# A fused attention and expert kernel whose hand-planned step list gets new durations and landing times

## The chip, the cores and the metric

The kernel runs on one core of one Trainium2 chip. The metric is the device time of one execution in microseconds. A profile of one execution gives the instructions of every engine: TensorE (PE, with its weight loads as PEld), VectorE (DVE), ScalarE (ACT), GpSimd (POOL) and SyncE (SP, which issues most transfers).

## The reference

Three parts follow one another, all in 32-bit floats.

```python
# attention: q, k, v are (4, 8, 576, 64)
kv = einsum('bhsd,bhse->bhde', k, v)
out = einsum('bhsd,bhde->bhse', q, kv)
out = out / sqrt(mean(out * out, -1) + 1e-06) * g_norm
x = out as (2304, 512)
# experts: 8 of them, one for each token
logits = (x / |x|) @ (expert_emb / |expert_emb|).T / tau
idx, gate = argmax(logits), softmax(logits)[idx]
x = gate * (relu(x @ w1[idx]) @ w2[idx])          # 512 -> 1024 -> 512
# dense layer
return softplus(x @ w_in) @ w_out                 # 512 -> 2048 -> 512
```

## The kernel before

The work falls into an attention stage, an expert stage and a dense stage, in this order. The change touches the attention stage alone.

The attention is cut into 18 tiles of 128 tokens (t = 0 to 17). Four batches (b = 0 to 3) give four tiles each, taken from the first 512 tokens of the batch, and two more tiles hold the last 64 tokens of two batches (t = 8 for batches 0 and 1, t = 13 for batches 2 and 3). So t = 0 to 3 are batch 0, 4 to 7 batch 1, 9 to 12 batch 2 and 14 to 17 batch 3. All loads of k, v and q are issued by SyncE ahead of the list, in the order in which they are used.

For each batch, TensorE forms the k-v product of its eight heads in two halves, `mm(b,0)` and `mm(b,1)` (`kv_mm`, 20 matmuls of lines 298 and 299 each half), and six short steps `fin(b,0)` to `fin(b,5)` (`kv_fin`) turn it into the operand of the output step. For each tile: `q` (VectorE copies q's columns, line 341), `tr` (TensorE transposes, line 347), `qs` (ScalarE copies the result out, line 350), `o` (TensorE multiplies with the k-v product, line 358, or line 362 for t = 8 and 13), `sq` and `cp` (ScalarE squares and copies, lines 365 and 372), and `ss` (VectorE sums the squares, line 375). For each pair of tiles: `rs` (ScalarE, Ln and Exp, lines 379 and 380), three Newton steps `n` (VectorE, lines 153 to 157), `lt` and `lg` (VectorE, logits, lines 387 and 395), then for each tile `xa` (GpSimd scales the tile, line 401, and SyncE stores it), `xo` (GpSimd, line 418, or VectorE, line 420) and `nn` (ScalarE, line 428). After t = 5, 11 and 17 a group of six tiles is routed: `top` (maximum), `slot` (places in the expert lists; `code` at line 468, selection at line 479), `red` and `acc` (counts), `tok` and `tab`; after the last group `rank` and `idx` give the indices with which the expert stage gathers its rows.

In which order each engine gets its steps is worked out by a planner while the kernel is built (`list_schedule`). Every step is entered with `step(key, engines, ns, fn, *deps, at=..., tail=...)`: `ns` is its assumed duration, `deps` the steps that must be over, `at` the earliest time at which it may start (for steps that need a load, from the table `LATE`, counted from the start of the list), and `tail` what follows it outside the list. The planner's core:

```python
lag = [end[d] + (220 if where[d] != eng else 0 if eng == "P" else 130) for d in deps]
t0 = max([free[eng], at] + lag)
...
t0, k0, eng, t1 = min(ready, key=lambda r: (r[0], -length(r[1])))
t0, k0, eng, t1 = max((r for r in ready if r[2] == eng and r[0] <= t0 + SLACK), key=lambda r: (length(r[1]), -r[0]))
```

`length` is the longest path of durations (with 180 for each step) from the step to the end of the list, and `SLACK` is 100. An `xo` step goes to GpSimd or VectorE, whichever would end it first. A step of kind `nn` or `xo` gives way to another step of its engine that could start before 0.8 of its duration has passed. The steps are then written out in the order of their planned start. Only the order reaches the chip: each engine runs its instructions in that order, and each waits for what it needs by semaphores. Two misplaced numbers can therefore delay a step, but not make it run on missing data.

The list starts behind the k-v product of batch 0 and the transposes of tiles 0 and 1, and ends with `idx`, `xo` and `nn` of the last tiles. Then come the offsets, the first gathers, the split of the first weights and the first expert's transposes, and after them eight experts and the dense layer.

Of the kernel before, what the change touches and what calls it, by code (L numbers as in the profile page):

```python
# [25 lines left out]
def attention_moe_mlp(tc, q, k, v, g_norm, emb, tau, w1, w2, w_in, w_out, out, caps=CAPS):  # L26
# [58 lines left out]
    NSQ = 4  # L85
# [102 lines left out]
    with ExitStack() as hs:  # L188
# [99 lines left out]
        def kv_mm(b, heads, whole=True):  # L288

            for h in heads:  # L290
                key = (b, 0 if whole else h // 4)
                j = h // 2 if whole else h % 4 // 2
                if key not in kvs:
                    kvs[key] = misc_t[:, 0:4 * D].rearrange("p (j d) -> p j d", d=D) if whole else o_t[h // 4][:, 0:2, 0:D]
                kvo = kvs[key][64 * (h % 2):64 * (h % 2) + 64, j, :]
                for c in range(4):
                    cs_ = slice(c * D, c * D + D)
                    nc.tensor.matmul(kvo, kt[b][:, h, cs_], vt[b][:, h, cs_], start=c == 0, stop=False)
                nc.tensor.matmul(kvo, kr[b][:, h, :], vr[b][:, h, :], start=False, stop=True)
# [38 lines left out]
        def st_q(t):  # L338

            lo, c = tiles[t]  # L340
            nc.vector.tensor_copy(qc_t[t % NQC], qt[lo][:, :, c, :])

        def st_tr(t):
            lo, c = tiles[t]
            src = qr[lo] if c is None else qc_t[t % NQC].rearrange("p h d -> p (h d)")
            for j in range(4):
                nc.tensor.transpose(qp_t[t % 2][:, j, :], src[:, 128 * j:128 * j + 128], ident)
# [4 lines left out]
        def st_o(t):  # L352

            lo, c = tiles[t]
            o, qs = o_t[t % 2], qs_t[t % NQS]
            for j in range(4):
                if c is not None:
                    nc.tensor.matmul(o[:, j, 0:144], qs[:, j, :], kvx[lo][:, j, :], start=True, stop=True)
                else:
                    for u in range(2):  # L360
                        us = slice(64 * u, 64 * u + 64)
                        nc.tensor.matmul(o[us, j, 0:144], qs[:, j, us], kvx[lo + u][:, j, :], start=True, stop=True)
# [64 lines left out]
        def st_n(t):  # L427
            nc.scalar.activation(out=junk, in_=xo_t[t % NXO], func=AF.Square, accum_out=ssx[:, t:t + 1])
# [165 lines left out]
        def step(key, engs, ns, fn, *deps, at=0, tail=0):  # L594

            steps_[key] = [engs, ns if isinstance(ns, tuple) else (ns,), fn, [d for d in deps if d in steps_], at, tail]

        LATE = {"kv1a": 3900, "kv1b": 7200, "q1": 10700, "kv2a": 15400, "kv2b": 18800, "qr0": 20100, "q2": 23500,
                "kv3a": 28200, "kv3b": 31600, "qr2": 32900, "q3": 36300}
        for b in range(1, B):  # L600
            step(("mm", b, 0), "P", 2350, lambda b=b: kv_mm(b, range(0, 4)), ("fin", b - 1, 5), at=LATE[f"kv{b}a"])
            step(("mm", b, 1), "P", 2350, lambda b=b: kv_mm(b, range(4, 8)), ("mm", b, 0), at=LATE[f"kv{b}b"])
            gen_ = kv_fin(b)
            mm = ("mm", b, 1)
            for i, (eng, ns, deps) in enumerate((
                ("A", 264, [mm]), ("D", 331, [mm]), ("P", 435, [("fin", b, 0), ("fin", b, 1)]),
                ("A", 478, [("fin", b, 2)]), ("P", 830, [("fin", b, 3)]), ("D", 131, [("fin", b, 4)]),
            )):
                step(("fin", b, i), eng, ns, lambda g_=gen_: next(g_), *deps)

        def route(g):
            a, z = groups[g]
            n = z - a
            last_ = g == NG - 1
            gen_ = top1(g)
            for i in range(5):
                step(("top", g, i), "D", 119, lambda g_=gen_: next(g_), *([("lg", p) for p in range(a // 2, z // 2)] if i == 0 else [("top", g, i - 1)]))
            oh = ("top", g, 4)
            gen_ = slots(g)
            prev = [oh, ("acc", g - 1), ("tab", g - 1)]  # L620
            for i, (eng, ns) in enumerate((("P", 250), ("D", 119), ("D", 119), ("D", 145), ("D", 145 * n), ("D", 37 * n + 10), ("D", 37 * n + 10), ("D", 37 * n + 10))):
                step(("slot", g, i), eng, ns, lambda g_=gen_: next(g_), *prev)
                prev = [("slot", g, i)]
            gen_ = count(g)
            step(("red", g), "D", 119, lambda g_=gen_: next(g_), oh)
            step(("acc", g), "D", 77, lambda g_=gen_: next(g_), ("red", g), ("slot", g, 0), ("acc", g - 1))
            gen_ = tokens(g)
            step(("tok", g), "P", 60 * n, lambda g_=gen_: next(g_), ("slot", g, 7), *([("qs", NT - 2)] if last_ else []))
            step(("tab", g), "D", 94, lambda g_=gen_: next(g_), ("tok", g), ("tab", g - 1))
            if last_:  # L630
                gen_ = ranks()
                prev = [("acc", g), ("fin", B - 1, 5)]
                for i, (eng, ns) in enumerate((("P", 30), ("D", 77), ("D", 135), ("D", 135), ("D", 135), ("D", 135), ("D", 135), ("D", 73))):
                    step(("rank", i), eng, ns, lambda g_=gen_: next(g_), *prev, tail=5000 if i == 6 else 0)
                    prev = [("rank", i)]
                gen_ = indices()
                step(("idx", 0), "D", 140, lambda g_=gen_: next(g_), ("tab", g), ("rank", 4), tail=6000)
                step(("idx", 1), "D", 140, lambda g_=gen_: next(g_), ("idx", 0), tail=6000)
                step(("idx", 2), "D", 370, lambda g_=gen_: next(g_), ("idx", 1), tail=3000)
                step(("idx", 3), "D", 350, lambda g_=gen_: next(g_), ("idx", 2), tail=3000)  # L640

        ends = {z - 1: g for g, (a, z) in enumerate(groups)}
        for t in range(NT):
            lo, c = tiles[t]
            p = t // 2
            if t > 1:
                if c is not None:
                    step(("q", t), "D", 335, lambda t=t: st_q(t), ("tr", t - NQC), at=LATE.get(f"q{lo}", 0))
                step(("tr", t), "P", 435, lambda t=t: st_tr(t), ("q", t), ("qs", t - 2), at=LATE[f"qr{lo}"] if c is None else 0)
                step(("qs", t), "A", 478, lambda t=t: st_qs(t), ("tr", t), ("o", t - NQS))  # L650
            step(("o", t), "P", 1180 if c is not None else 1500, lambda t=t: st_o(t), ("qs", t), ("fin", lo if c is not None else lo + 1, 5), ("cp", t - 2), ("sq", t - 2), ("o", t - 1))
            step(("sq", t), "A", 478, lambda t=t: st_sq(t), ("o", t), ("ss", t - NSQ))
            step(("cp", t), "A", 531, lambda t=t: st_cp(t), ("o", t), ("lt", p - NOC), ("xa", 2 * (p - NOC)), ("xa", 2 * (p - NOC) + 1))
            step(("ss", t), "D", 610, lambda t=t: st_ss(t), ("sq", t), ("n", p - NSS, 2))
            if t % 2:
                step(("rs", p), "A", 460, lambda p=p: st_rs(p), ("ss", t - 1), ("ss", t), ("n", p - NSS, 2))
                gen_ = st_newton(p)
                for i in range(3):
                    step(("n", p, i), "D", 85, lambda g_=gen_: next(g_), ("rs", p) if i == 0 else ("n", p, i - 1), ("xa", 2 * (p - NSS)), ("xa", 2 * (p - NSS) + 1))
                step(("lt", p), "D", 202, lambda p=p: st_lt(p), ("n", p, 2), ("cp", t - 1), ("cp", t), ("lg", p - 2))  # L660
                step(("lg", p), "D", 202, lambda p=p: st_lg(p), ("lt", p))
                for u in (t - 1, t):
                    step(("xa", u), "G", 1001, lambda u=u: st_xa(u), ("n", p, 2), ("cp", u), ("xa", u - 1), tail=12000 if u == NT - 1 else 0)
                for u in (t - 1, t):
                    if u < NXD:
                        step(("xo", u), "GD", (1225, 560), lambda eng, u=u: st_xo(u, eng), ("xa", u), ("nn", u - NXO))
                        step(("nn", u), "A", 613, lambda u=u: st_n(u), ("xo", u))
            if t in ends:
                route(ends[t])
        for u in range(NXD, NT):  # L670
            step(("xo", u), "D", 700, lambda u=u: st_xo(u, "D"), ("idx", 3), ("xa", u), ("nn", u - NXO))
            if u < NT - 3:
                step(("nn", u), "A", 613, lambda u=u: st_n(u), ("xo", u))

        def list_schedule():

# [812 lines left out]
```

## Time and profile before

| what | value |
| --- | --- |
| time, median of 3 runs | 737.45 us (734.54 to 738.94) |
| the profiled execution's own time | 735.82 us |
| its span, first to last instruction | 734.0 us |
| TensorE busy | 705.5 us, 96% of the span |
| VectorE busy | 519.9 us, 71% |
| ScalarE busy | 406.9 us, 55% |
| GpSimd busy | 262.8 us, 36% |
| mean granted TensorE clock | 0.986 of full speed |

The span is 1.8 us shorter than the time of the same execution. Shares of the whole span say little about a change to the attention stage, which takes about the first ninth of it; the rows further down are cut by stretches for that reason. In the first of them a line gives the stretch in us from the span's start, its length, then for each engine its busy us with the number of instructions behind an x, the granted clock, the mean busy share of the DMA engines (transfers that overlap count twice, so it can pass 1), and what they moved.

### The profile page before, as it was taken

Reading aid. Unit: us, or ns where it says so; the run is one execution under the profiler, and the core shown is the slowest. Engines: PE = TensorE matmul, PEld = TensorE weight load, DVE = VectorE, ACT = ScalarE, POOL = GpSimd, SP = SyncE. Lnnn points to the kernel's source line nnn. Section 1 sums busy time; section 2 is a strip of 40 time slices with the busy share of each in tenths; the row PEclk is TensorE's granted clock in tenths of the full one; section 3 lists DMA queues with packets and bytes.
Section 4 is the critical chain, followed back from the end, with each engine's and each line's share of the span. In section 5 each row is a group of like instructions: output and inputs, shape, how many; then the busy total and the mean of one; then the engine's idle time right before and its main releaser. Section 6 shows DMA issues by size and latency. Waiting matters only on the chain. (4 is left out here: it accounts for less than half of the span.)

```text
span 734.0 us, 11456 instructions
## 1 busy us (share of the span) xinstructions
PE 705.5 (96%) x4195; PEld 618.0 (84%) x4195; DVE 519.9 (71%) x947; ACT 406.9 (55%) x754; POOL 262.8 (36%) x200
## 2 busy tenths in 40 slices
PE   7987699999999999999999999999999999999995
PEld 4886399999999999998888888888888888888894
DVE  5489888878879789886887756557565665566563
ACT  1779466666657656555665554446443554445553
POOL 5244339767686787672552020001100020000201
PEclk8999799999999999999999999999999999999999
DMA  8995598899898898821130010000100010000100
GB/s 245 276 251 194 170 351 289 296 303 282 273 305 289 288 314 277 295 65 58 58 115 1 1 57 1 1 0 15 44 1 1 0 52 7 0 1 1 57 1 33
DMA packets 66912, 96.66 MB, mean 132 GB/s; under 512 B 12948, under 2 KB 41644, under 8 KB 66850
## 3 DMA queue, kind: packets, MB, share of 16 engines
q1 hardware_dynamic: 63330, 86.02, 37.8%
q0 software_dynamic: 3344, 9.80, 3.7%
q8 instruction: 35, 0.57, 0.4%
q14 instruction: 27, 0.22, 0.1%
q10 hardware_dynamic: 176, 0.05, 0.0%
HBM read 78.01 MB, written 17.84 MB: 131 GB/s over the span
## 5 line engine op out<-in xcount | busy, mean ns | idle before, releaser
L887 POOL TENSOR_TENSOR wl<-st,wh 128x1024 fp32r<-128x1024 f32 x64 | 156.4, 2447 | 58.7 <-ACT wh L885 56.6
L992 POOL DMA_INDIRECT out_dram<-orow,idx x18 | 18.4, 1025 | 317.2 <-ACT orow L991 314.2
L955 DVE TENSOR_SCALAR u<-e 128x512 f32<-128x512 f32 (+1 forms) x78 | 31.1, 399 | 123.6 <-ACT e L954 123.5
L953 ACT ACTIVATE e<-tp_t 128x512 f32<-128x512 f32 (+1 forms) x76 | 42.5, 559 | 128.0 <-PE tp_t L881 127.9
L885 ACT CAST wh<-st 128x1024 fp32r<-128x1024 f32 x72 | 74.8, 1046 | 38.9 <-PE acc_t L880 15.5
L879 PE MATMUL acc_t<-hh,wh 128*128 128x368 f32 (+7 forms) x256 | 81.1, 317 | 0.0
L879 PE MATMUL acc_t<-xh,wh 128*128 128x368 f32 (+7 forms) x256 | 78.5, 307 | 1.0 <-ACT x L1334 0.5
L881 PE MATMUL acc_t<-hh,wl 128*128 128x368 f32 (+7 forms) x256 | 78.1, 305 | 0.9 <-DVE wl L887 0.9
L880 PE MATMUL acc_t<-xl,wh 128*128 128x368 f32 (+7 forms) x256 | 78.2, 305 | 0.0
L881 PE MATMUL acc_t<-xh,wl 128*128 128x368 f32 (+7 forms) x256 | 78.0, 305 | 0.0
L880 PE MATMUL acc_t<-hl,wh 128*128 128x368 f32 (+7 forms) x256 | 78.0, 305 | 0.0
L961 ACT ACTIVATE u<-u 128x512 f32<-128x512 f32 (+1 forms) x78 | 46.0, 590 | 43.9 <-DVE e L957 43.2
L880 PE MATMUL tp_t<-xs,wh 128*128 128x512 f32 (+1 forms) x160 | 59.0, 368 | 0.4 <-DVE xs L897 0.4
L974 DVE TENSOR_TENSOR gl<-u,gh 128x512 fp32r<-128x512 f32 (+1 forms) x78 | 56.8, 729 | 3.0 <-ACT gh L973 3.0
L881 PE MATMUL tp_t<-xs,wl 128*128 128x512 f32 (+1 forms) x160 | 58.9, 368 | 0.0
L879 PE MATMUL tp_t<-xs,wh 128*128 128x512 f32 (+1 forms) x160 | 58.8, 368 | 0.0
L1005 PE MATMUL acc_t<-wh,gl 128*128 128x512 f32 x144 | 56.2, 391 | 0.9 <-DVE gl L974 0.9
L1003 PE MATMUL acc_t<-wh_b,gh 128*128 128x512 f32 x144 | 56.2, 390 | 0.6 <-ACT gh L973 0.6
L881 PE MATMUL tp_t<-xs,wl_b 128*128 128x512 f32 (+1 forms) x152 | 56.6, 372 | 0.0
L880 PE MATMUL tp_t<-xs,wh_b 128*128 128x512 f32 (+1 forms) x152 | 56.6, 372 | 0.0
L879 PE MATMUL tp_t<-xs,wh_b 128*128 128x512 f32 (+1 forms) x152 | 56.6, 372 | 0.0
L1003 PE MATMUL acc_t<-wh,gh 128*128 128x512 f32 x144 | 56.1, 390 | 0.0
(268 smaller groups left out, 1817.6 us busy)
## 6 DMA issues: line engine op xcount, KB each, us to landing
st<-in_moe_w_dram SPq DMA_DIRECT2D x64, 512.0 KB
raw<-in_moe_w_in_dram SPq DMA_DIRECT2D x16, 512.0 KB
raw<-in_moe_w_out_dram SPq DMA_DIRECT2D x16, 512.0 KB
wd<-pre_p SPq DMA_DIRECT2D x32, 256.0 KB
q<-in_q_dram SPq DMA_DIRECT2D x4, 1024.0 KB
xd<-xa SPq DMA_DIRECT2D x16, 256.0 KB
st<-wd SPq DMA_DIRECT2D x8, 512.0 KB
raw<-wd SPq DMA_DIRECT2D x8, 512.0 KB
```

What stands on the lines that cost most here:

```text
L879: nc.tensor.matmul(ps_, wh, xh, start=start, stop=False)
L880: nc.tensor.matmul(ps_, wh, xl, start=False, stop=False)
L881: nc.tensor.matmul(ps_, wl, xh, start=False, stop=stop)
L885: nc.scalar.copy(h, raw)
L887: eng.tensor_tensor(out=l, in0=raw, in1=h.bitcast(F32), op=ALU.subtract)
L953: nc.scalar.activation(out=e, in_=h, func=AF.Abs)
L955: nc.vector.tensor_scalar(out=u, in0=e, scalar1=1.0, scalar2=None, op0=ALU.add)
L961: nc.scalar.activation(out=u, in_=u, func=AF.Ln)
L974: nc.vector.tensor_tensor(out=gl, in0=u, in1=gh.bitcast(F32), op=ALU.subtract)
L992: nc.gpsimd.indirect_dma_start(out=rows_out[i], out_offset=bass.IndirectOffsetOnAxis(ap=idx2[:, i:i + 1], axis=0), in_=o, in_offset=None)
L1003: nc.tensor.matmul(mt[b][t_], gh[:, cs_], wh[:, f % 2, :], start=f == 0, stop=False)
L1005: nc.tensor.matmul(mt[b][t_], gl[:, cs_], wh[:, f % 2, :], start=False, stop=f == NF - 1)
```

## The change

The numbers that the planner is given are replaced: the table `LATE` of landing times, and the assumed durations of most steps. The table has earlier landings up to the second half of batch 3's k and v (`kv3b`) and the last pair of remainders (`qr2`), and a slightly later one for batch 3's q. The assumed duration of the k-v halves goes down, that of most short VectorE steps goes up by half or doubles, and others move by less than a fifth. Every step, its dependences, tiles and buffers stay as they are; the order in which engines are given the steps, and the engine that an `xo` step is put on, follow from the planner.

```diff
-        LATE = {"kv1a": 3900, "kv1b": 7200, "q1": 10700, "kv2a": 15400, "kv2b": 18800, "qr0": 20100, "q2": 23500,
-                "kv3a": 28200, "kv3b": 31600, "qr2": 32900, "q3": 36300}
+        LATE = {"kv1a": 800, "kv1b": 4300, "q1": 7600, "kv2a": 12100, "kv2b": 16100, "qr0": 17300, "q2": 21800, "kv3a": 26800, "kv3b": 31000, "qr2": 32100, "q3": 36500}
...
-            step(("mm", b, 0), "P", 2350, lambda b=b: kv_mm(b, range(0, 4)), ("fin", b - 1, 5), at=LATE[f"kv{b}a"])
-            step(("mm", b, 1), "P", 2350, lambda b=b: kv_mm(b, range(4, 8)), ("mm", b, 0), at=LATE[f"kv{b}b"])
+            step(("mm", b, 0), "P", 2050, lambda b=b: kv_mm(b, range(0, 4)), ("fin", b - 1, 5), at=LATE[f"kv{b}a"])
+            step(("mm", b, 1), "P", 2050, lambda b=b: kv_mm(b, range(4, 8)), ("mm", b, 0), at=LATE[f"kv{b}b"])
...
-                ("A", 264, [mm]), ("D", 331, [mm]), ("P", 435, [("fin", b, 0), ("fin", b, 1)]),
-                ("A", 478, [("fin", b, 2)]), ("P", 830, [("fin", b, 3)]), ("D", 131, [("fin", b, 4)]),
+                ("A", 264, [mm]), ("D", 331, [mm]), ("P", 600, [("fin", b, 0), ("fin", b, 1)]),
+                ("A", 478, [("fin", b, 2)]), ("P", 960, [("fin", b, 3)]), ("D", 170, [("fin", b, 4)]),
```

The other durations, in ns, before and after: `top` 119 each, now 230, 300, 230, 240, 230; `slot` 250, 119, 119, 145 for its first four, now 400, 210, 230, 330 (the rest stay); `red` 119, now 200; `acc` 77, now 110; `rank` 30, 77, 135 five times, 73, now 100, 110, 200 five times, 130; the first two `idx` 140, now 190; `q` 335, now 400; `tr` 435, now 500; `o` 1180 and 1500 (t = 8, 13), now 1120 and 1200; `sq` 478, now 500; `rs` 460, now 540; `n` 85, now 190; `lt` 202, now 310; `lg` 202, now 350; `xo` 1225 on GpSimd and 560 on VectorE, now 1280 and 610; `nn` 613, now 730.

## Rows read from the trace of the kernel before

**Rows 1.** Busy time by stretch: length, PE, PEld, DVE, ACT, POOL, clock, DMA share, GB/s.
```profile
21.28:30.30 9.02, 9.02 (x121) 8.57 (x121) 4.75 (x12) 6.20 (x14) 2.86 (x3) 1.00 1.12 317
30.30:40.00 9.70, 9.13 (x102) 8.19 (x102) 6.93 (x20) 8.48 (x21) 2.65 (x4) 1.00 1.17 244
40.00:50.00 10.00, 9.43 (x134) 8.61 (x130) 8.22 (x28) 7.70 (x18) 5.31 (x6) 1.00 1.15 260
50.00:57.10 7.10, 5.73 (x74) 5.40 (x73) 5.54 (x15) 4.51 (x12) 2.08 (x2) 1.00 1.15 273
57.10:66.00 8.90, 6.98 (x76) 6.54 (x74) 8.56 (x22) 7.36 (x18) 4.86 (x6) 1.00 0.63 237
66.00:75.70 9.70, 5.51 (x53) 4.53 (x52) 9.53 (x26) 7.76 (x21) 5.48 (x5) 1.00 0.34 110
75.70:84.20 8.50, 4.50 (x29) 1.88 (x29) 6.86 (x34) 0.48 (x2) 2.49 (x3) 0.50 0.30 112
...
91.60:734.00 642.40, 631.82 (x3466) 558.87 (x3466) 452.72 (x751) 353.49 (x626) 222.77 (x120) 1.00 0.36 118
```

**Rows 2.** Timeline of TensorE at the list's start: start us, us, instructions.
```profile
21.28 2.24 PE L358 MATMUL o<-kvx,qs 128*128 128x144 f32 x16
...
24.32 0.73 PE L298 MATMUL misc<-v,k 128*64 128x64 f32 x10
...
26.26 1.25 PE L358 MATMUL o<-kvx,qs 128*128 128x144 f32 x8
```

**Rows 3.** Timeline of VectorE: copies of q and sums of squares.
```profile
30.65 1.42 DVE L341 COPY qc<-q 128x512 f32<-128x512 f32 x4
...
57.08 3.12 DVE L341 COPY qc<-q 128x512 f32<-128x512 f32 x3 [0.24 <-DMA q<-in_q_dram]
60.12 0.68 DVE L375 TENSOR_REDUCE ss<-sqb 128x8 f32<-128x520 f32 x1
...
74.94 0.68 DVE L375 TENSOR_REDUCE ss<-sqb 128x8 f32<-128x520 f32 x1
```

**Rows 4.** Timeline of ScalarE: the last square and the last Ln of the list.
```profile
72.06 0.58 ACT L365 ACTIVATE sqb<-o 128x512 f32<-128x512 f32 x1
...
75.66 0.22 ACT L379 ACTIVATE r<-ss 128x16 f32<-128x16 f32 x1 [1.87 <-DVE ss L375]
```

**Rows 5.** Timeline of TensorE, 34 to 60 us.
```profile
34.17 2.23 PE L358 MATMUL o<-kvx,qs 128*128 128x144 f32 x16
36.33 0.73 PE L298 MATMUL misc<-v,k 128*64 128x64 f32 x10
...
47.80 0.66 PE L298 MATMUL misc<-v,k 128*64 128x64 f32 x8
48.60 0.24 PE L299 MATMUL misc<-vr,kr 128*64 128x64 f32 x1
...
50.14 1.25 PE L358 MATMUL o<-kvx,qs 128*128 128x144 f32 x8
52.76 0.70 PE L298 MATMUL misc<-v,k 128*64 128x64 f32 x10 [1.37 <-DMA v<-in_v_dram]
...
57.36 2.21 PE L358 MATMUL o<-kvx,qs 128*128 128x144 f32 x16
```

**Rows 6.** Timeline of GpSimd, 56 to 60 us.
```profile
56.23 2.27 POOL L401 TENSOR_TENSOR xa<-oc,rinv 128x512 f32<-128x512 f32 x2 [5.02 <-DVE rinv L157]
58.58 1.34 POOL L418 TENSOR_TENSOR xo<-xa,g_rep 128x512 f32<-128x512 f32 x1
```

**Rows 7.** VectorE's copies of q in the list: shortest, median, longest in ns.
```profile
L341 DVE COPY qc<-q x14: 408/416/1498, 21.6 to 62.7; 128x512 f32<-128x512 f32 x14
```

**Rows 8.** Timeline of VectorE: three short steps; the third needs the first.
```profile
67.18 0.21 DVE L468 TENSOR_TENSOR code<-rt,oh_all 128x48 f32<-128x48 f32 x1
67.31 0.15 DVE L512 TENSOR_TENSOR acc<-acc,red 128x8 bf16<-128x8 bf16 x1
67.42 0.20 DVE L472 TENSOR_REDUCE ci<-code 128x6 int32<-128x48 f32 x1
```

More of the change, by code (lines that the diff above doesn't have):

```diff
@@ L615, in route @@
             gen_ = top1(g)
-            for i in range(5):
-                step(("top", g, i), "D", 119, lambda g_=gen_: next(g_), *([("lg", p) for p in range(a // 2, z // 2)] if i == 0 else [("top", g, i - 1)]))
+            for i, ns in enumerate((230, 300, 230, 240, 230)):
+                step(("top", g, i), "D", ns, lambda g_=gen_: next(g_), *([("lg", p) for p in range(a // 2, z // 2)] if i == 0 else [("top", g, i - 1)]))
             oh = ("top", g, 4)
@@ L620, in route @@
             prev = [oh, ("acc", g - 1), ("tab", g - 1)]
-            for i, (eng, ns) in enumerate((("P", 250), ("D", 119), ("D", 119), ("D", 145), ("D", 145 * n), ("D", 37 * n + 10), ("D", 37 * n + 10), ("D", 37 * n + 10))):
+            for i, (eng, ns) in enumerate((("P", 400), ("D", 210), ("D", 230), ("D", 330), ("D", 145 * n), ("D", 37 * n + 10), ("D", 37 * n + 10), ("D", 37 * n + 10))):
                 step(("slot", g, i), eng, ns, lambda g_=gen_: next(g_), *prev)
@@ L624, in route @@
             gen_ = count(g)
-            step(("red", g), "D", 119, lambda g_=gen_: next(g_), oh)
-            step(("acc", g), "D", 77, lambda g_=gen_: next(g_), ("red", g), ("slot", g, 0), ("acc", g - 1))
+            step(("red", g), "D", 200, lambda g_=gen_: next(g_), oh)
+            step(("acc", g), "D", 110, lambda g_=gen_: next(g_), ("red", g), ("slot", g, 0), ("acc", g - 1))
             gen_ = tokens(g)
@@ L632, in route @@
                 prev = [("acc", g), ("fin", B - 1, 5)]
-                for i, (eng, ns) in enumerate((("P", 30), ("D", 77), ("D", 135), ("D", 135), ("D", 135), ("D", 135), ("D", 135), ("D", 73))):
+                for i, (eng, ns) in enumerate((("P", 100), ("D", 110), ("D", 200), ("D", 200), ("D", 200), ("D", 200), ("D", 200), ("D", 130))):
                     step(("rank", i), eng, ns, lambda g_=gen_: next(g_), *prev, tail=5000 if i == 6 else 0)
@@ L636, in route @@
                 gen_ = indices()
-                step(("idx", 0), "D", 140, lambda g_=gen_: next(g_), ("tab", g), ("rank", 4), tail=6000)
-                step(("idx", 1), "D", 140, lambda g_=gen_: next(g_), ("idx", 0), tail=6000)
+                step(("idx", 0), "D", 190, lambda g_=gen_: next(g_), ("tab", g), ("rank", 4), tail=6000)
+                step(("idx", 1), "D", 190, lambda g_=gen_: next(g_), ("idx", 0), tail=6000)
                 step(("idx", 2), "D", 370, lambda g_=gen_: next(g_), ("idx", 1), tail=3000)
@@ L647, in attention_moe_mlp @@
                 if c is not None:
-                    step(("q", t), "D", 335, lambda t=t: st_q(t), ("tr", t - NQC), at=LATE.get(f"q{lo}", 0))
-                step(("tr", t), "P", 435, lambda t=t: st_tr(t), ("q", t), ("qs", t - 2), at=LATE[f"qr{lo}"] if c is None else 0)
+                    step(("q", t), "D", 400, lambda t=t: st_q(t), ("tr", t - NQC), at=LATE.get(f"q{lo}", 0))
+                step(("tr", t), "P", 500, lambda t=t: st_tr(t), ("q", t), ("qs", t - 2), at=LATE[f"qr{lo}"] if c is None else 0)
                 step(("qs", t), "A", 478, lambda t=t: st_qs(t), ("tr", t), ("o", t - NQS))
-            step(("o", t), "P", 1180 if c is not None else 1500, lambda t=t: st_o(t), ("qs", t), ("fin", lo if c is not None else lo + 1, 5), ("cp", t - 2), ("sq", t - 2), ("o", t - 1))
-            step(("sq", t), "A", 478, lambda t=t: st_sq(t), ("o", t), ("ss", t - NSQ))
+            step(("o", t), "P", 1120 if c is not None else 1200, lambda t=t: st_o(t), ("qs", t), ("fin", lo if c is not None else lo + 1, 5), ("cp", t - 2), ("sq", t - 2), ("o", t - 1))
+            step(("sq", t), "A", 500, lambda t=t: st_sq(t), ("o", t), ("ss", t - NSQ))
             step(("cp", t), "A", 531, lambda t=t: st_cp(t), ("o", t), ("lt", p - NOC), ("xa", 2 * (p - NOC)), ("xa", 2 * (p - NOC) + 1))
@@ L655, in attention_moe_mlp @@
             if t % 2:
-                step(("rs", p), "A", 460, lambda p=p: st_rs(p), ("ss", t - 1), ("ss", t), ("n", p - NSS, 2))
+                step(("rs", p), "A", 540, lambda p=p: st_rs(p), ("ss", t - 1), ("ss", t), ("n", p - NSS, 2))
                 gen_ = st_newton(p)
                 for i in range(3):
-                    step(("n", p, i), "D", 85, lambda g_=gen_: next(g_), ("rs", p) if i == 0 else ("n", p, i - 1), ("xa", 2 * (p - NSS)), ("xa", 2 * (p - NSS) + 1))
-                step(("lt", p), "D", 202, lambda p=p: st_lt(p), ("n", p, 2), ("cp", t - 1), ("cp", t), ("lg", p - 2))
-                step(("lg", p), "D", 202, lambda p=p: st_lg(p), ("lt", p))
+                    step(("n", p, i), "D", 190, lambda g_=gen_: next(g_), ("rs", p) if i == 0 else ("n", p, i - 1), ("xa", 2 * (p - NSS)), ("xa", 2 * (p - NSS) + 1))
+                step(("lt", p), "D", 310, lambda p=p: st_lt(p), ("n", p, 2), ("cp", t - 1), ("cp", t), ("lg", p - 2))
+                step(("lg", p), "D", 350, lambda p=p: st_lg(p), ("lt", p))
                 for u in (t - 1, t):
@@ L665, in attention_moe_mlp @@
                     if u < NXD:
-                        step(("xo", u), "GD", (1225, 560), lambda eng, u=u: st_xo(u, eng), ("xa", u), ("nn", u - NXO))
-                        step(("nn", u), "A", 613, lambda u=u: st_n(u), ("xo", u))
+                        step(("xo", u), "GD", (1280, 610), lambda eng, u=u: st_xo(u, eng), ("xa", u), ("nn", u - NXO))
+                        step(("nn", u), "A", 730, lambda u=u: st_n(u), ("xo", u))
             if t in ends:
@@ L672, in attention_moe_mlp @@
             if u < NT - 3:
-                step(("nn", u), "A", 613, lambda u=u: st_n(u), ("xo", u))
+                step(("nn", u), "A", 730, lambda u=u: st_n(u), ("xo", u))
         def list_schedule():
```

## The prediction

> **What bounds the kernel now.** I read the table of busy time by stretch first [rows 1]. From 91.60 us on TensorE is busy 631.82 of 642.40 us. The change touches nothing there, so that stretch can only shift as a block. The list that the diff reorders runs from the first output step at 21.28 us [rows 2] to the indices that start the expert stage, near 84.2 us; then come 7.4 us (to 91.6) of gather, transposes and splits that hang on those indices. So the end moves as far as the last indices move, one for one.
>
> Inside the list three limits follow one another. Up to 57.1 us the loads are the limit: the DMA share stands at 1.12 to 1.17 in all four stretches, while VectorE idles 4.27, 2.77, 1.78 and 1.56 us in them (length minus busy) [rows 1]. The copies of the last block of q begin at 57.08 us, released by a DMA [rows 3]. From 57.1 to 75.7 us VectorE is the limit: busy 8.56 of 8.90 and 9.53 of 9.70 us, while TensorE has 1.92 and 4.19 us free and ScalarE 1.54 and 1.94 us [rows 1]. After that one chain is left. The last pair's Ln waits 1.87 us for VectorE's last sum of squares, which starts only at 74.94 us though ScalarE's square was written by about 72.64 us (72.06 + 0.58) [rows 3, 4]. What counts is therefore how much VectorE work is still undone at 57.1 us, and what slows it after that.
>
> **What the change does to the order.** No instruction is added, removed or resized. What moves is the place of a step in its engine's queue. I followed the planner's rule by hand (earliest start, then the longest remaining path, engines in order) with the new numbers, on TensorE, taking the other engines as not late. I use it for the order alone; times come from rows. Plan zero is 21.28 us of the trace.
>
> *Start.* `kv1a` now lands at 800, not 3900. When o(0) ends, at 1120, mm(1,0) is ready and has by far the longest remaining path (three k-v blocks in series), so it goes ahead of tr(2), tr(3) and o(1). One half of a k-v block takes 1.94 us (24.32 to 26.26) and o(1), which ran right behind o(0) [rows 2], gets tr(2) before it too (500 ns in the diff): o(1) comes some 2.5 us later. VectorE has nothing else then; it idles 4.27 us in that stretch already [rows 1]. By the same rule mm(2,0) (12100) comes before o(4), where the list before ran o(4) and o(5) first, at 34.17, and mm(2,0) at 36.33 [rows 5]: o(4) and o(5) come about 1.6 us later (half a block, 1.94, less 0.3 us by which block 1's finish is earlier).
>
> *Block 2.* mm(2,1) at 16100 instead of 18800 lets block 2 finish earlier; q2 lands at 21800, and o(9) is ready in the plan at about 26400, just before `kv3a` at 26800. The list before put mm(3,0) first: TensorE then starts it at 47.80, is held inside it till 48.60, and gives o(9) only at 50.14; then mm(3,1) holds the queue 1.37 us for its load at 52.76, so o(11) and o(12) run at 57.36 [rows 5]. With o(9) ahead of mm(3,0), it can start near 46.9 us: 3.2 us earlier. o(10) fits between the two halves of block 3 and gains some 3.5 us, o(11) some 2.2, o(12) some 1.1. The same rows test the landings: 26800 and 31000 from 21.28 are 48.08 and 52.28, where the trace shows 48.60 and 52.76, so the new numbers are about 0.5 us early and right in their order.
>
> **What that is worth, by terms.** The stretch from 57.08 us holds about 18.6 us of VectorE almost without a pause (57.08 to 75.62, where the last sum of squares ends) [rows 1, 3]. (a) Its first three copies take 3.12 us instead of 3 x 0.34 (four in a row took 1.42 us at 30.65, and one alone 0.41, so each further one 0.34) [rows 3, 7]: they run beside GpSimd's scaling of tiles 8 and 9 (56.23, 2.27 us) and its tile product (58.58, 1.34 us), and the slowest copy took 1498 ns against a median of 416 [rows 6, 7]. With o(9) 3.2 us earlier that GpSimd work is over by about 56.7 us (59.92 less 3.2), before the copies start: 2.1 us back. If tiles 10 and 11 come in its place, nothing. Bounds 0 and 2.1. (b) The sum of squares of tile 10 (60.12) goes ahead of 57 us: 0.68 us as recorded [rows 3], of which I count 0.6, since the next step starts before the end that is recorded (below). Bounds 0 and 0.6. (c) Against it, the work of block 1 that comes 1.6 us later must fit into the idle that is left before 57.1 us. In the three stretches from 30.3 us there are 2.77 + 1.78 + 1.56 = 6.11 us of it [rows 1], more than 1.6 plus the 2.5 of the late start; I take a loss of 0.5, bounds 0 and 2.5. (d) The last sum of squares could start 2.3 us sooner (74.94 against 72.64) [rows 3, 4] if nothing else had to be done first; but the second group's routing must be done before the third's, so I count 0.3, bounds 0 and 2.3.
>
> Sum: -2.1 - 0.6 + 0.5 - 0.3 = -2.5 us. The bounds add up to -5.0 and +2.5. Everything else in the diff (TensorE, ScalarE and GpSimd durations changed by under a fifth) I take at nothing: it decides ties, and TensorE and ScalarE have 1.5 to 4.2 us free in the stretches that count [rows 1]. Were that cover gone, one k-v half in a wrong place would cost its 1.94 us.
>
> **Small VectorE steps.** The new numbers take a step's whole recorded duration, 190 to 350 ns. In the trace `code` starts at 67.18 and lasts 0.21 us, yet an independent step starts 0.13 us behind it, and the step that needs `code` 0.24 us behind it [rows 8]. The planner adds 130 ns between dependent steps of one engine, so it now books 210 + 130 = 340 ns where 240 pass; before it booked 119 + 130 = 249. Counted over the list (27 Newton steps at +105, 15 of the maximum at about +127, 18 of lt and lg at +128, 14 copies at +65, the rest some 2 us) VectorE is booked about 10 us fuller than before. The order of its steps is then that of an engine later than the true one, and more `xo` steps go to GpSimd, each 0.6 us less for VectorE. The Trainium skill, Perfetto Trace Analysis, section "Optimizing Scalar/DVE Operations", says that a profiled latency is about twice the busy time, since the write acknowledgement overlaps the next instruction; the trace agrees (0.21 against 0.13). By that rule alone the old numbers were the better ones and the term is a loss, which is the third rival below.
>
> **The rivals.** *The whole backlog goes* (faster by over 3.7 us): terms (a), (b), (d) at their full size, -5.0, and no loss: 735.82 - 5.0 = 730.8 in this execution's terms. For it: VectorE's 6.11 us of idle ahead of 57 us. Against: the routing that must precede the last pair. *The start starves* (the other side): o(1) and o(4) late make VectorE begin later, its idle in 30.3 to 57.1 us turns out to be waits within chains that can't be filled, and the stretch from 57.1 us gets it all: 2.5 + 1.6 = +4.1, 739.9; it decides as soon as under 4.1 of those 6.11 us can be filled and GpSimd's work still meets the copies. *The bookings mislead*: VectorE's queue has a late step ahead of an early one at several places, and GpSimd takes more products that meet copies; each meeting costs 1498 - 416 = 1.08 us and saves 0.6. Three such meetings and the lost gain (a) leave +1.4, 737.2. The skill's rule above is what speaks for it. *Nothing comes of it* (the loads and the last block's own work set the end, and what is gained ahead of 57 us is waited for there): 735.8.
>
> **How the numbers follow.** The profiled execution took 735.82 us beside its span of 734.0; the median of the runs is 737.45, 1.63 higher, so -2.5 from the median is 735.0. Chances: forecast (-0.5 to -3.7 us) 0.34, whole backlog 0.31, nothing 0.08, bookings mislead 0.09, start starves 0.18. What a measurement can tell from no change is 0.5%, 3.7 us: faster 0.33 (the whole backlog and a little of the forecast), slower 0.18 (most of the starved start, some of the misled bookings), within it 0.49. From the median the cases reach from 737.45 - 5.0 = 732.4 to 737.45 + 4.1 = 741.6; for 8 in 10, and the 2 us by which single runs spread, 731.0 to 740.5; the likeliest case alone 733.7 to 737.
>
> **What would show it.** Right: the first k-v matmuls of block 1 directly behind o(0); o(9) ahead of mm(3,0); no GpSimd scaling across the copies of q3, which then take near 1 us; VectorE's idle growing in 21 to 30 us and shrinking in 40 to 57; the indices near 81.5 us and the first expert matmul near 89. Wrong: copies of q3 still over 2 us; TensorE held for a load where it was not before (a landing taken too early by more than the 0.5 us seen); VectorE waiting between 57 and 75 us, which would mean that its queue, not its load, is the limit there. The stretch behind the first expert matmul should last 642 us as before; if it doesn't, the reason lies outside the list.

## The result, and the profile after

The changed kernel is slower: 741.26 us median of 6 runs (739.22 to 741.65) against 737.2 for the kernel before (6 runs). The ratio is 1.0057, with a 95% interval of 1.0034 to 1.008, or 4.2 us. The forecast was 735.0, and the time lies 0.8 us above the range. The profiled execution took 741.52 us (span 739.7).

The busy time by stretch of the changed kernel answers [rows 1]: length, PE, PEld, DVE, ACT, POOL, clock, DMA share, GB/s.

```profile
21.28:30.30 9.02, 9.02 (x116) 8.58 (x116) 2.73 (x7) 4.94 (x11) 0.00 (x0) 0.90 1.11 318
...
40.00:50.00 10.00, 6.93 (x73) 6.40 (x69) 9.14 (x23) 6.54 (x17) 5.09 (x5) 1.00 1.16 249
50.00:57.10 7.10, 6.99 (x76) 6.50 (x77) 3.78 (x12) 4.33 (x12) 5.31 (x5) 0.76 1.09 312
57.10:66.00 8.90, 8.90 (x101) 8.41 (x97) 5.97 (x17) 8.57 (x22) 2.62 (x3) 1.00 0.48 171
66.00:75.70 9.70, 5.66 (x58) 4.50 (x56) 8.98 (x27) 8.45 (x22) 7.35 (x7) 0.92 0.34 109
```

Three things have moved. From 40 to 50 us TensorE loses 2.5 us (9.43 to 6.93) and ScalarE 1.2 (7.70 to 6.54), while VectorE is fuller (8.22 to 9.14). From 50 to 66 us VectorE is busy 9.75 us instead of 14.10 (3.78 + 5.97 against 5.54 + 8.56): it now waits for others. And from 57.1 us TensorE (8.90 of 8.90) and ScalarE (8.57) are full, where before they had 1.92 and 1.54 us free: the work they missed between 40 and 57 us is done there.

The hole between 40 and 50 us, in the timelines of the changed kernel (start us, us, instruction, in brackets the idle time before it and what ended it). VectorE, the copies of block 2's q and the sum behind them:

```profile
43.41 4.45 DVE L341 COPY qc<-q 128x512 f32<-128x512 f32 x4
47.78 0.68 DVE L375 TENSOR_REDUCE ss<-sqb 128x8 f32<-128x520 f32 x1
```

GpSimd beside them:

```profile
42.31 2.08 POOL L401 TENSOR_TENSOR xa<-oc,rinv 128x512 f32<-128x512 f32 x2 [3.80 <-DVE rinv L157]
44.35 2.89 POOL L418 TENSOR_TENSOR xo<-xa,g_rep 128x512 f32<-128x512 f32 x2
```

ScalarE, where line 379 is the Ln of pair 3, and line 350 behind it copies out tile 9's transposed q:

```profile
44.62 0.69 ACT L372 COPY oc<-o 128x576 f32<-128x576 f32 x1
48.49 0.22 ACT L379 ACTIVATE r<-ss 128x16 f32<-128x16 f32 x1 [3.19 <-DVE ss L375]
...
48.96 0.62 ACT L372 COPY oc<-o 128x576 f32<-128x576 f32 x1
49.48 0.59 ACT L350 COPY qs<-qp 128x512 f32<-128x512 f32 x1
```

TensorE, with o(9) and the first half of block 3:

```profile
45.84 1.09 PE L347 MATMUL qp<-ident,qc 128*128 128x128 f32 x8
50.12 2.12 PE L358 MATMUL o<-kvx,qs 128*128 128x144 f32 x8 [3.18 <-ACT qs L350]
52.16 1.18 PE L298 MATMUL misc<-v,k 128*64 128x64 f32 x10
```

Read from the top down. The four copies take 4.45 us; before they took 1.42, from 43.35. They run beside the scaling of tile 5 (the second of the two at 42.31) and the products 4 and 5 (`xo`), where in the kernel before GpSimd had ended product 4 at 43.22, just ahead of them, and product 5 was VectorE's work. So the sum of tile 7's squares comes 3 us late, the Ln of pair 3 waits 3.19 us for it at the head of ScalarE's queue, and the copy of tile 9's q stands behind that Ln though its transposes were over at 46.93 (45.84 + 1.09). TensorE, with o(9) ahead of `mm(3,0)`, stands 3.18 us. Tile 9 itself needs nothing from that Ln. The granted clock of the stretch from 50 us, behind this pause, is 0.76, a mixture of the levels of 1.2 and 2.4 GHz (1.00 before), and o(9) takes 2.12 us instead of 1.25 [rows 5].

The copies of block 3's q, by contrast, are free of GpSimd's work, as forecast ([rows 3]: 3.12 us for the first three):

```profile
59.71 0.41 DVE L341 COPY qc<-q 128x512 f32<-128x512 f32 x1
61.71 0.69 DVE L375 TENSOR_REDUCE ss<-sqb 128x8 f32<-128x520 f32 x1 [1.59 <-ACT sqb L365]
62.32 0.75 DVE L341 COPY qc<-q 128x512 f32<-128x512 f32 x2
...
63.81 0.42 DVE L341 COPY qc<-q 128x512 f32<-128x512 f32 x1
```

At the end of the list the indices are ready at 88.16 us (87.83 + 0.33), before at 84.15. The first expert matmul starts at 98.01, before at 91.64, and the stretch behind it lasts 641.7 us (739.7 - 98.01), before 642.4:

```profile
87.83 0.33 DVE L558 TENSOR_REDUCE rk_idx<-pt 128x21 int32<-128x168 f32 x1
```

```profile
93.31 0.63 PE L1131 MATMUL acc_t<-ident,xgt 128*128 128x128 f32 x4 [2.00 <-DMA xgt<-xd,rk_idx]
...
98.01 0.47 PE L878 MATMUL acc_t<-xh,wh 128*128 128x368 f32 x1 [0.45 <-ACT xh L1135]
```

So the 5.7 us between the two spans are: o(0) 1.1 later (22.41 against 21.28; it lay between 17.7 and 22.4 us in the profiles of this study), from o(0) to the indices 2.9 more, from the indices to the first expert matmul 2.4 more (9.85 against 7.49), behind it 0.7 less. Of these 2.4 us, 1.1 lie ahead of the first transposes, which wait for the gathered rows (they start 5.15 us behind the indices instead of 4.03), and 1.2 between them and the first expert matmul (4.70 us instead of 3.46). In that last piece the granted clock is 0.65 in this profile and 1.00 in those of all the other kernels here, and the same four transposes take longer; first the changed kernel, then the kernel before:

```profile
94.43 0.90 PE L1131 MATMUL acc_t<-ident,xgt 128*128 128x128 f32 x4
```

```profile
89.08 0.60 PE L1132 MATMUL acc_t<-ident,xgt 128*128 128x128 f32 x4
```

### The profile page after: what moved, and what is told of

It is laid out like the page before. It is cut to its first block, busy times and chain, and to the rows that moved or that the text cites. A ratio compares the mean times of both kernels' runs of the same rounds, so it can differ in the third digit from the quotient of the medians.

```text
span 739.7 us, 11470 instructions
## 1 busy us (share of the span) xinstructions
PE 708.8 (96%) x4195; PEld 621.3 (84%) x4195; DVE 515.7 (70%) x945; ACT 407.3 (55%) x754; POOL 267.2 (36%) x202
## 5 line engine op out<-in xcount | busy, mean ns | idle before, releaser
L1003 PE MATMUL acc_t<-wl,gh 128*128 128x512 f32 x144 | 56.1, 390 | 0.0
```

The lines of the kernel that those rows point to most:

```text
L1003: nc.tensor.matmul(mt[b][t_], gh[:, cs_], wl[:, f % 2, :], start=False, stop=False)
```

## The experiments

The theories at the outset: the products that GpSimd now gets meet the copies of block 2's q; VectorE's fuller bookings put its steps in a worse order (the first group's routing, line 460, comes at 67.38 us instead of 47.33); o(9) ahead of `mm(3,0)` makes TensorE stand. Ratios are to the kernel before on the same chip.

**Which numbers.** Parts of the change, put on the kernel before. *All but VectorE's*: the durations of engine "D" as before, and likewise the converse.

```diff
-                step(("n", p, i), "D", 190, ...
+                step(("n", p, i), "D", 85, ...
```

> All new numbers but VectorE's, which stay as before. The planner then puts the first group's routing on TensorE before the second half of block 2 is used up (slot(0,0) ahead of o(9)), as before the change; o(1) still comes behind the first half of block 1, and 8 products go to GpSimd (5 before, 7 after the change). Late routing as the cause: the 2.5 us of VectorE work leave the last stretch, and block 2 keeps its lead: 735 to 738 us, ratio to before 0.997 to 1.001. Starved start as the cause: 740 to 742, as the start is the same as after the change. Products on GpSimd as the cause: 741 or more, as there are more of them.

Measured (e1): 737.1 us, ratio 1.0000 (0.9985 to 1.0015). GpSimd gets eight products, three copies of block 2's q take 3.67 us, and the Ln of pair 3 waits 3.53 us behind them:

```profile
49.43 0.22 ACT L379 ACTIVATE r<-ss 128x16 f32<-128x16 f32 x1 [3.53 <-DVE ss L375]
```

By its expectation this speaks for late routing and against the products. The runs below (e3, e12 and e8) decide otherwise: the collision costs here too, and something else gains as much.

> Only VectorE's numbers are new; landing times and the other engines are as before. TensorE's order at the start is that of before, slot(0,0) stays ahead of block 3, 7 products go to GpSimd. Late routing as the cause: no loss, 736.5 to 738.5. Starved start: none here, 737. Overfull bookings of VectorE or products on GpSimd as the cause by themselves: 739.5 to 741.5.

Measured (e2): 737.61 us, 1.0016 (0.9996 to 1.0036), copies of block 2's q 1.43 us. VectorE's numbers alone don't make the whole loss; it needs the others too. Whether they make a small part of it, this interval leaves open.

**Routing.** The changed kernel with the first group's routing put back to early places, written behind the planner:

```diff
         begin, where = list_schedule()
+        for k, at in ((("slot", 0, 0), 27620), (("slot", 0, 1), 31700), ..., (("acc", 0), 34530), (("tok", 0), 35485), (("tab", 0), 36400)):
+            begin[k] = at
```

> The changed kernel with its list as it is, but the first group's routing from slot(0,0) to tab(0) is put forward: slot(0,0) on TensorE right behind the first half of block 3, the VectorE steps into the idle that VectorE has at 55 to 58 us. Late routing as the cause: VectorE has 2.5 us less to do behind 57 us, and the second group's routing no longer waits for the first: 2.5 to 4 us faster than the changed kernel, 737.5 to 739. Starved start or products on GpSimd: 741, unchanged.

Measured (e3): 741.4 us, 1.0055 (1.0031 to 1.0078). Its selection (line 479) runs at 58.03 us instead of 69.67, and nothing is gained. The test is not a clean one, since VectorE now stands 2.64 us for the routing matmul at 54.67; with e12 below, which has the early places without the slow copies, it speaks against this theory.

**Products.** The changed kernel with the engine of each product given, first as in the kernel before, then with 4 and 5 alone on VectorE, then with 10 and 11:

```diff
-                        step(("xo", u), "GD", (1280, 610), lambda eng, u=u: st_xo(u, eng), ...
+                        step(("xo", u), *(("G", 1280) if u in (1, 4, 6, 9, 11) else ("D", 610)), lambda u=u: st_xo(u, "G" if u in (1, 4, 6, 9, 11) else "D"), ...
```

> The changed kernel, but the products go to the engines that they were on before the change (5 on GpSimd in place of 7, none at 44 to 47 us beside the copies of block 2's q). Products on GpSimd as the cause: the copies at 43 us take 2 to 3 us less than their 4.45 and o(9) starts that much earlier: 738 to 739. Late routing as the cause: what is gained at 43 us is waited for again before the end, 740 to 742. Starved start: 741.

Measured (e4): 737.73 us, 1.0014 (0.9997 to 1.003); copies 3.15 us, wait at the Ln 2.12. The copies give back only 1.3 us, less than expected, as product 4 still meets them, and yet no loss can be told any more.

> The changed kernel, but products 4 and 5, which GpSimd ran at 44.35 to 47.24 us beside the copies of block 2's q, go to VectorE, where the planner puts them some 5 to 7 us later; GpSimd keeps the other five. Collision at the copies of block 2 as the cause: the copies take about 2.5 us in place of 4.45 (the scaling of tile 5 still meets them), o(9) and block 3's k-v follow some 2 us earlier, 737 to 739 us. Collisions at the end (products 10 and 11) as the cause: unchanged, 741.

Measured (e5): 736.15 us, 0.9989 (0.9976 to 1.0003). The whole loss is gone. VectorE and TensorE of this kernel:

```profile
43.76 2.28 DVE L341 COPY qc<-q 128x512 f32<-128x512 f32 x4
45.97 0.68 DVE L375 TENSOR_REDUCE ss<-sqb 128x8 f32<-128x520 f32 x1
```

```profile
48.30 1.25 PE L358 MATMUL o<-kvx,qs 128*128 128x144 f32 x8 [1.01 <-ACT qs L350]
```

> The changed kernel, but products 10 and 11, which GpSimd ran at 66.71 to 69.24 us, go to VectorE close to the end of the list; products 4 and 5 stay on GpSimd beside the copies of block 2's q. Collisions at the end as the cause: 738 to 739 us. Collision at the copies of block 2 as the cause: 740.5 to 742, with the copies still at about 4.45 us.

Measured (e6): 739.56 us, 1.0046 (1.0021 to 1.007), with copies of 4.44 us and a wait of 3.18 us at the Ln. In microseconds that lies between the two forecasts; as a ratio it fits the second (740.5 over the 737.2 of the kernel before is 1.0045). Two products fewer on GpSimd don't help where they are not the two at the copies. It is the place of the products, not their number.

**A collision in the other list.** The kernel before with product 5 moved to GpSimd by the same edit.

> The kernel before with one change: product 5 goes to GpSimd, right behind product 4, where it meets the copies of block 2's q (43.35 to 44.77 us). Nothing else in the list moves. Collision at these copies as the cause: the copies take 1 to 2 us longer and the kernel becomes 1 to 2 us slower than before, 738 to 739. If the time between there and the end of the list absorbs it: 736.5 to 737.5.

Measured (e7): 736.57 us, 0.9997 (0.9982 to 1.0012). The copies take 2.95 us instead of 1.42 and the Ln waits 0.19: in that order 1.5 us of VectorE are absorbed, half of what the copies cost in the changed kernel. And, by that edit, the e1 kernel with products 4, 5 and 6 on VectorE:

> All new numbers but VectorE's (as in e1_vector_old, 737.1 us), and products 4, 5 and 6 on VectorE instead of GpSimd, so that no product meets the copies of block 2's q. Collision at these copies as the cause: 2 to 3 us faster than e1_vector_old, 734 to 735.5, faster than both kernels. If VectorE's load counts for more: 737 to 738, since it gets 1.8 us of products back.

Measured (e8): 732.96 us, 0.9949 (0.993 to 0.9969), copies 1.50 us for three: faster than both kernels.

**o(9) and block 3.** The changed kernel with `begin["mm", 3, 0] = begin["o", 9] - 1`, and the kernel before with the converse, without and with product 5 on GpSimd:

> The changed kernel with one step moved: on TensorE the first half of block 3's k-v goes ahead of o(9), as it stood before the change. The products on GpSimd stay where the change put them, so the copies of block 2's q still take about 4.45 us. If the loss comes from o(9), held back by these copies, keeping block 3's k-v waiting behind it in TensorE's queue: 736.5 to 738.5 us, as before. If the slow copies cost by themselves: 740 to 742.

Measured (e9): 740.15 us, 1.0068 (1.0043 to 1.0093). `mm(3,0)` starts at 47.96 instead of 52.16 (5.2 us behind the start of the copies instead of 8.8), behind a pause of 1.71 us for VectorE's line 323 instead of one of 3.18 at o(9); o(9) starts at 49.90, and the Ln still waits 3.19 us. TensorE and ScalarE of this kernel:

```profile
47.96 0.73 PE L298 MATMUL misc<-v,k 128*64 128x64 f32 x10 [1.71 <-DVE kvx L323]
```

```profile
47.81 0.22 ACT L379 ACTIVATE r<-ss 128x16 f32<-128x16 f32 x1 [3.19 <-DVE ss L375]
```

That o(9) holds block 3 up in TensorE's queue is not the cause.

> The kernel before with one step moved: o(9) ahead of the first half of block 3's k-v on TensorE, which is the change's step on which most of the prediction rested. No product meets the copies of block 2's q. As predicted, a gain: 734 to 736 us. If the lead of o(9) is worth nothing by itself: 736 to 737.5.

Measured (e10): 736.07 us, 1.0009 (0.9994 to 1.0024). o(9) starts at 46.02 us, 4.1 earlier than in [rows 5]. In this profile the whole list began 3.5 us earlier (17.80); counted from the start of block 2's copies, o(9) comes after 3.8 us instead of 6.8, so the lead is 3.0 us. It is worth nothing.

> The kernel before with both: o(9) ahead of block 3's k-v, and product 5 on GpSimd beside the copies of block 2's q (which alone cost nothing in e7_before_collide, 736.6 us, though the copies took 2.95 us in place of 1.42). If the two cost only together: 737.5 to 739, slower than each alone. If they don't act on each other: the time of e10_before_o9_first.

Measured (e11): 736.64 us, 1.0012 (0.999 to 1.0035). The copies took only 1.71 us here, so the collision was a small one, and whether the two cost together is not tested by it.

> The changed kernel without products 4 and 5 on GpSimd (e5_no_products_q2, 736.2 us), and with the first group's routing put forward into VectorE's idle ahead of the last block (as in e3_routing_early, where it gave nothing while the copies were slow). If late routing costs once block 3 is no longer late: 733 to 735 us. If it costs nothing at all: 736.

Measured (e12, the kernel of e5 with the early routing): 736.23 us, 1.0000 (0.9984 to 1.0017): nothing, with a wait of 1.69 us at VectorE for the routing matmul.

**ScalarE's queue.** (The same edit follows on e5 and on e1.) What remained open was how 3 us of copying become a loss of 4 to 5 us. The changed kernel, products and all, with one step moved:

```diff
         begin, where = list_schedule()
+        begin["rs", 3] = begin["qs", 10] + 1
```

> The changed kernel with one ScalarE step moved: the Ln and Exp of pair 3, in the changed list ahead of the copy-out of o(8) and of the transposed q of tile 9, go behind the copy-out of the transposed q of tile 10. GpSimd keeps all seven products, two of them beside the copies of block 2's q. Theory A (the lost 5 us come from the 3.19 us that ScalarE's queue, and behind it TensorE, stands at that Ln): o(9) starts at 47.0 to 48.0 us instead of 50.12 and the ratio to the kernel before falls to 0.999 to 1.002. Theory B (what is lost is VectorE time in the copies, whoever waits for it): the copies still take 4.2 to 4.5 us, o(9) moves up, and the ratio stays at 1.004 to 1.007, since the sum and all VectorE steps behind the copies are as late as before.

Measured (e13): 736.98 us, 1.0007 (0.9994 to 1.0021), against 1.0057. VectorE, ScalarE and TensorE of this kernel (its profiled execution, 739.97 us, was the slowest of its 12, so only the order of things is read from it):

```profile
43.61 4.46 DVE L341 COPY qc<-q 128x512 f32<-128x512 f32 x4
```

```profile
46.75 0.59 ACT L350 COPY qs<-qp 128x512 f32<-128x512 f32 x1
...
49.94 0.21 ACT L379 ACTIVATE r<-ss 128x16 f32<-128x16 f32 x1 [1.61 <-DVE rinv L157]
```

```profile
48.95 1.22 PE L358 MATMUL o<-kvx,qs 128*128 128x144 f32 x8 [1.81 <-DVE kvx L323]
```

The copies are as long as ever, and nearly all of the loss is gone. Theory A has the ratio, and theory B's 1.004 to 1.007 is excluded. Theory A missed one thing: o(9) came at 48.95, not by 48.0. ScalarE delivers tile 9's q on time, and the next thing late is line 323, the last step of block 2's finish, which stands behind the same sum in VectorE's queue.

> The same ScalarE move, in the kernel whose products 4 and 5 are on VectorE (0.9989 without the move). Theory A: a wait of 1.02 us is left to take away there, ratio 0.996 to 0.998. Theory B: no change that can be measured, 0.998 to 1.000.

Measured (e16): 734.88 us, 0.9983 (0.9968 to 0.9998). The point lies in theory B's range, and theory A's forecast of a gain was missed, though the interval allows either. Against e5's 0.9989 that is no difference that can be told; nothing shows that the wait of 1.02 us was worth its length.

> All new numbers but VectorE's (1.0000 so far, with an Ln of pair 3 that waits 3.53 us for the sum behind the copies of block 2's q), with that Ln put behind the copy-out of tile 10's transposed q. There a routing matmul of the first group stands ahead of o(9) in TensorE's queue too and waits for VectorE till 49.69, so o(9) can come from 51.05 only to about 49.9. If the wait at the Ln is the whole price, 0.995 to 0.997; if the second wait holds o(9) in its place, 0.998 to 1.000. The first reading of VectorE's copies, 3.7 us for three, should stay.

Measured (e17): 735.86 us, 0.9998 (0.9979 to 1.0017): no gain. ScalarE now copies tile 9's q out at 47.08, and o(9) comes at 49.79 all the same, as expected of the second wait. In this list a routing matmul stands ahead of o(9) and waits for VectorE work behind the copies, on TensorE's timeline:

```profile
49.41 0.18 PE L460 MATMUL rt<-oh_all,upper 128*128 128x48 bf16 x1 [2.27 <-DVE oh_all L451]
49.79 1.95 PE L358 MATMUL o<-kvx,qs 128*128 128x144 f32 x8
```

**Landings and TensorE's durations, each alone** (the table `LATE`; the durations of `mm`, `tr`, `o`, `fin` and of the routing's matmuls), and then TensorE's with VectorE's:

> The kernel before with the new landing moments alone, every duration as before. GpSimd then gets the products 4, 8, 9 and 10, so one product may meet the copies of block 2's q. If the landings alone bring the start order and nothing of the loss, ratio 0.995 to 1.001 with copies of block 2's q at 1.4 to 3 us. If the landings are what brings the loss, 1.003 to 1.006.

Measured (e14): 738.26 us, 1.0023 (1.0005 to 1.0042), between the two forecasts. The four copies of block 2's q take 1.60 us, so what loss there is doesn't come from them; those of block 3 still take 3.17.

> The kernel before with the new TensorE durations alone, landings and the rest as before. GpSimd then gets the products 1, 4, 6, 7, 9 and 11. If TensorE's shorter durations bring the gain that the fastest variant so far showed (0.995), ratio 0.994 to 0.997; if landings and durations are needed together, 0.998 to 1.002.

Measured (e15): 732.53 us, 0.9946 (0.993 to 0.9963), the fastest here. Its copies of q meet nothing in either block, so the 2.1 us that term (a) wanted at block 3 are there; how much of the gain they are was not tested:

```profile
43.53 1.44 DVE L341 COPY qc<-q 128x512 f32<-128x512 f32 x4 [1.03 <-DMA q<-in_q_dram]
...
57.45 1.43 DVE L341 COPY qc<-q 128x512 f32<-128x512 f32 x4 [0.88 <-DMA q<-in_q_dram]
```

> The new TensorE and VectorE durations, landings and the rest as before. TensorE's alone gave 0.9946. GpSimd then gets the products 1, 4, 5, 7, 10 and 11 and the first group's selection goes behind 43 us of the plan. If VectorE's fuller bookings cost what they cost beside the landings (0.4 to 0.6%), 0.998 to 1.001, with one or two products on the copies of block 2's q; if they cost only together with the landings, 0.993 to 0.996.

Measured (e18): 734.92 us, 0.998 (0.9961 to 1.0), at the edge of the first forecast; three copies of block 2's q took 1.87 us.

## Why the prediction was wrong, step by step

**The step that failed** is the sentence "more `xo` steps go to GpSimd, each 0.6 us less for VectorE", together with the choice to follow the planner "on TensorE, taking the other engines as not late". The count was right (GpSimd has seven products instead of five), but where they would lie was not followed. Products 4 and 5 lie on block 2's copies. Term (a) had priced just this meeting, at block 3's copies; there it did go, and it came back 16 us earlier, as 4.45 - 1.42 = 3.0 us. The third rival, "the bookings mislead", had the mechanism, with a chance of 0.09, and was sized too low: it counted VectorE's time alone (1.08 us each, 0.6 back, net +1.4 with the lost gain), and nothing for what is queued behind. Removing the two products gives back 0.0068 (1.0057 to 0.9989), 5.0 us; moving one ScalarE step past the wait gives back 0.0050, 3.7 us, with the copies unchanged (each give or take 2 us by the intervals). So in this list most of the price is not the copying but what stands behind it in ScalarE's in-order queue.

**Which engine's standing still costs.** e9 and e13 leave TensorE nearly the same pause (1.71 and 1.81 us, both for line 323), but in e9 ScalarE stands 3.19 us at the Ln, and in e13 it copies tile 9's q out meanwhile. e9 stayed slow, e13 was cured. So in this list the pair points to ScalarE's standing still, with what waits behind it. It is not a rule for every list: in e1 the Ln waits 3.53 us and the kernel is at 1.0000, 0.5% behind the same list with three products taken off GpSimd (e8), and taking the wait at the Ln away (e17) gave nothing. There TensorE stands 2.26 us for VectorE at the routing matmul as well. Little room is left later for what is missed: from 57.1 us ScalarE is busy 8.57 of 8.90 and TensorE 8.90, and VectorE waits there for ScalarE's squares (1.59 us at 61.71). In e7's order the Ln waits only 0.19 us, and a collision half as long is free. How ScalarE's lost 3.19 us go on to the last indices was not followed as one chain. The kernels in which the Ln waits over 3 us (the changed one, e1, e3, e6, e9) also need 7.8 to 9.9 us from the indices to the first expert matmul, the others 7.3 to 7.8. That the prediction took this piece as fixed ("one for one") was wrong in this profile. It doesn't mark the slow kernels, since e1 is among the five, and why it grows is open.

**Start.** Right: the first matmuls of block 1 run directly behind o(0), o(1) comes at 26.30, and VectorE is busy 2.73 us instead of 4.75 up to 30.3 us. o(4) comes at 36.39, 2.2 us later than in [rows 5]; 1.1 of that is the later start of the whole list, so 1.1 stand against the forecast of 1.6. Term (c)'s small loss is not excluded, but e8 has this start and is at 0.9949: it can be absorbed. "The start starves" is not what happened.

**Block 2.** Right in order, o(9) is ahead of `mm(3,0)`; wrong in time, 50.12 instead of 46.9. The lead itself, the core of the forecast gain, is worth nothing: with it in the list before (e10), 1.0009. Term (b) and (d) therefore had nothing to stand on; the sums behind 57 us waited for ScalarE.

**Everything else at nothing.** Wrong the other way. TensorE's durations, which I took as deciding ties, are the part that gains: alone 0.9946. Landings, which carried the forecast, are alone 1.0023. The prediction named the loads alone as the limit up to 57.1 us; the same rows show TensorE busy 9.02 of 9.02, 9.13 of 9.70 and 9.43 of 10.00 us up to 50 us [rows 1], so TensorE had little room there either. By which steps its durations gain was not followed.

**Small VectorE steps.** Three pairs with and without VectorE's new numbers: 1.0057 and 1.0000, 0.9989 and 0.9949 (products at the copies removed; not the same set of products elsewhere), 0.998 and 0.9946. The new numbers are on the worse side each time, by 0.3 to 0.6%, and in the first two pairs the intervals don't meet. On the kernel before they change nothing that can be told (e2, 1.0016). The worse side is the one that the prediction expected from the Trainium skill, Perfetto Trace Analysis, section "Optimizing Scalar/DVE Operations", by which a profiled latency is about twice the time that the engine is busy; no run shows that this is the reason. The late routing does not seem to be the way in which it costs (e3, e12); which step is, stays open.

**What held.** The stretch behind the first expert matmul, 641.7 against 642.4 us. In the list of the changed kernel TensorE waits for no load. Two of the signs came as well: the copies of block 3's q take 1.6 us for four, a sign of being right, and VectorE waits between 57 and 75 us, a sign of being wrong.

## What to carry to other kernels

When a planner may choose the engine of a step, follow where the step lands in time, not only how many there are: a VectorE copy and a GpSimd operation at the same moment can cost more than the move saves (nothing in e7's order, some 5 us in the changed one). Price a late result by what is queued behind the instruction that waits for it: here an Ln that could run later held up a copy that TensorE waited for, and moving it by four steps undid most of the loss. And replace a planner's numbers one kind at a time; one kind here was worth 0.5%, and all together cost 0.6%.

## What was not expected of the hardware

Three of the four copies each lasted about as long as one GpSimd operation: the longest took 1511 ns of a median of 418, and the two products beside them 2.89 us together. The view of VectorE's copies in the changed kernel, shortest, median and longest in ns:

```profile
L341 DVE COPY qc<-q x16: 407/418/1511, 17.8 to 63.8; 128x512 f32<-128x512 f32 x16
```

GpSimd pays too: two products took 2.53 us at 66.71, so each at the copies is about 0.18 us longer. A sum of squares beside GpSimd's scaling kept its 0.69 us (42.79, scaling from 42.31). That fits the Trainium skill, SBUF — State Buffer, section "Who interferes with whom": copies can take the port pair that VectorE shares with GpSimd, and whoever comes second is blocked for the whole of the other's instruction, while a tensor reduce never contends. Short steps of 128x16 elements were hit as well: on VectorE, while GpSimd scaled or multiplied tiles,

```profile
68.31 0.97 DVE L153 TENSOR_TENSOR r<-r 128x16 f32<-128x16 f32 x1
...
73.49 0.16 DVE L153 TENSOR_TENSOR r<-r 128x16 f32<-128x16 f32 x1
74.41 0.95 DVE L153 TENSOR_TENSOR r<-r 128x16 f32<-128x16 f32 x1
```

The one at 73.49 ran while GpSimd stood (its scalings ended at 72.58 and began at 74.29): 0.16 us alone, 0.95 beside it. A planner that books such a step at one duration can't see this.

The lower clock between 50 and 57.1 us does not account for the loss: e9 kept 1.00 there and was slow (1.0068), and e1 had 0.76 and was at 1.0000. The stretch in e9:

```profile
50.00:57.10 7.10, 6.45 (x75) 6.03 (x76) 5.20 (x14) 5.96 (x15) 5.69 (x6) 1.00 1.12 296
```
